# Output projection of a two-branch attention: split float32r products per row block, against float32 pieces of 128 columns behind P @ V

## The chip, the cores and the metric

The kernel runs on one NeuronCore of one Trainium2 chip. The metric is device time in microseconds (us), the median of several executions. The engines named here are TensorE (PE, its weight loads PEld), VectorE (DVE), ScalarE (ACT), GpSimd (POOL) and SyncE (SP), which issues nearly all DMAs. PSUM has eight banks, each of 128 partitions by 512 float32 columns.

## What is computed

The input is `x` with 2048 rows of 512, 32 heads of width 16. Branch A is plain softmax attention, branch B works on four chunks of 512 rows, causal inside a chunk, and mixes in a running memory of earlier chunks. Both have an output projection, and a gate mixes them:

```python
# A
p = softmax(q @ k.T * scale);  a = (p @ v) @ A_wo
# B, for each chunk s of 512 rows
a_dot = softmax(qs @ ks.T * scale + mask) @ vs
a_mem = (phi(qs) @ M) / (phi(qs) @ z + 1e-6)
o_s = sigmoid(beta) * a_mem + (1 - sigmoid(beta)) * a_dot
M, z = M + phi(ks).T @ vs, z + phi(ks).sum()
b = concat(o_s) @ B_wo
# both
g = sigmoid((x * gate_w).sum(-1));  out = g * a + (1 - g) * b
```

## The kernel before

**Stage 0** (lines 277 to 550) computes Q, K and V of both branches, the memory numerators and denominators of branch B, and the gates, and stores them in DRAM. At its end it also begins the row maxima.

**The slot loop** (lines 910 to 933) is all the rest. The work is cut into 64 units (`units`, line 99): side A or B, a group of four heads, a chunk of 512 query rows. A unit of side A has 64 slots, one of side B 10, 2368 slots in all, and 32 pairs of an A and a B unit of 74 slots each. One turn of the loop is one slot n and emits:

- `score_part(n)` (line 606): one score product into a bank of pool `st` (three banks), and ScalarE's exponential of that bank into a tile `p` (line 642, for two shapes 639).
- `max_part(n + 96)` (line 207): the product for the row maxima of a slot 96 later, into a bank of pool `sm` (four banks), and VectorE's reduction of that bank (line 219; for side B also 240, 244, and 230 to 234 by way of ScalarE and GpSimd). Score and maximum use different halves of the array's rows (heads at partitions 0 and 64), so a pair of them overlaps.
- every third slot (`BURST`), a burst: `some_values` (line 654) multiplies finished blocks of `p` by V. P @ V accumulates in one bank, `ops`, in float32, in four column tiles of the array: head h writes partitions 32h to 32h+16. A block is 128 query columns; up to four neighbours are one run of matmuls, so a run of w blocks is 4 heads x 128w columns, and each float32 matmul is two instructions. After it `run_late` (line 257) puts the transposed negated maxima into the query tile.

The program is written out by hand in this order. Each engine runs its own instructions in that order, so a matmul that waits for a bank holds everything behind it on TensorE.

**Beside it** stand steps given to a slot with `at(n, f)`. When a chunk of a side is done, its sums are loaded, inverted on VectorE, multiplied by the gate, stored, and loaded again as a factor broadcast over 16 partitions (`factors_at`, line 776; `value_load`, `factor_load`); GpSimd scales the values (`scale_part`, line 727) and adds the memory part (`memory_add`). The memory part is scaled ahead, stored to DRAM (`amd`) and loaded again.

**The projection** of chunks 0 to 2 is done per block of 128 rows. ScalarE makes the high part of the values in float32r (`out_hi`, 742), GpSimd the low part (`out_lo`, 747), for each side. `wo` was split the same way. Then `out_products` (line 750) makes 24 matmuls of 128x512 in three runs of eight (`RUN`), each into a bank of the score pool `st`, evacuated by ScalarE (760) and added by GpSimd (765). Each run of eight takes the place of P @ V in one burst (lines 926 to 932); the P @ V that was put off follows in the next. There are 4 blocks x 3 chunks x 3 = 36 such runs.

**The last chunk** goes by octets of eight heads (`piece`, line 834): six matmuls at a time into the four `sm` banks (line 890), in the last 88 or so slots, where there are no maxima any more. The octet of side A that ends last runs after the loop: its chain of DMAs, scale, split, 12 products and four copies out end the program.

Of the kernel before, what the change touches and what calls it, by code (L numbers as in the profile page):

```python
# [10 lines left out]
F32 = mybir.dt.float32  # L11
F32R = mybir.dt.float32r
# [25 lines left out]
RUN = 8  # L38
# [8 lines left out]
def gated_mix(ctx, tc, x, xT, wqkv, a_wo, b_wq, b_wk, b_wv, b_wo, beta, gate_w, out):  # L47
# [18 lines left out]
    amd = {c: dr.tile([128, NO, CH], F32, name=f"amd{c}") for c in range(1, NCH)}  # L66
# [18 lines left out]
    ogh = const.tile([128, 1], F32, name="ogh")  # L85
# [121 lines left out]
    def max_part(m, pool):  # L207
# [6 lines left out]
        ps = pool.tile([128, CH], F32, tag="sm", name="sm")  # L214
# [63 lines left out]
    with ExitStack() as p0:  # L278
# [145 lines left out]
        bt4 = wk1.tile([128, 1], F32, tag="bt4", name="bt4")  # L424
        nc.gpsimd.dma_start(bt4, beta.unsqueeze(1).unsqueeze(2).broadcast_to([H, 4, 1]))
# [87 lines left out]
        def some_max(place):  # L513
            m = mnext[0]
            if m == LEAD:
                return
            loads(m + 1 + PRE)
            for i in range(2):
                max_part(m + i, me_sm)
            run_todo(m + 1)  # L520
            mnext[0] += 2
            run_late(me_ps, "me", mnext[0])
# [31 lines left out]
    gate = {(s, c): gp.tile([128, 128], F32, name=f"g{s}{c}") for s in "AB" for c in range(NCH)}  # L554
    for (s, c), t in gate.items():
        nc.gpsimd.dma_start(t, gd["AB".index(s), c * CH:(c + 1) * CH].rearrange("(b t) -> b t", t=128)
                            .unsqueeze(0).broadcast_to([H, 4, 128]))
    gate_last = gp.tile([128, 32], F32, name="gateL")
    nc.gpsimd.dma_start(gate_last, gd[0, (NCH - 1) * CH:].rearrange("(q t) -> q t", q=16).unsqueeze(0).broadcast_to([8, 16, 32]))
# [6 lines left out]
    hl = ctx.enter_context(tc.tile_pool(name="hl", bufs=2, reuse_waits="tile"))  # L566
# [9 lines left out]
    def load_wo(side, w, t0):  # L576
        def load():
            wos["raw"] = fr.tile([128, NO, D], F32, tag="raw", name="woraw")
            nc.sync.dma_start(wos["raw"], w.rearrange("(o p) d -> p o d", p=128))
            wos[side] = [wo.tile([128, NO, D], F32R, name=f"wo{t}{side}") for t in "hl"]  # L580

        def split(o):
            h, l = wos[side]
            nc.gpsimd.tensor_copy(h[:, o], wos["raw"][:, o])
            nc.gpsimd.tensor_sub(l[:, o], wos["raw"][:, o], h[:, o].bitcast(F32))
        at(t0, load)
        for o in range(NO):
            at(t0 + 5 + 2 * o, lambda o=o: split(o))
# [13 lines left out]
    pt_ = {}  # L602

# [50 lines left out]
    def some_values(n, most=8):  # L654

        while queue and most and queue[0][0] <= n:
# [20 lines left out]
            if done:  # L677
                raw = ob.tile([128, CH], F32, tag="o", name="oraw")
                nc.scalar.copy(raw, ops)  # L679
                nc.sync.dma_start(od[side, c][4 * g:4 * g + 4].rearrange("h r t -> (h r) t"), raw)  # L680
                return


    held = {}

    def invert_load(side, c, src):
        t = fr.tile([128, 128], F32, tag="rec", name="rec", bufs=2)
        nc.sync.dma_start(t, src)
        held["rec", side, c] = t

    def recip(side, c, i, n=4):
        t = held["rec", side, c][:, i * 128 // n:(i + 1) * 128 // n]
        nc.vector.reciprocal(t, t)

    def invert(side, c):

        t = held.pop(("rec", side, c))
        if side == "B":
            nc.vector.scalar_tensor_tensor(t, t, ogh, gate["B", c], op0=ALU.mult, op1=ALU.mult)
        else:  # L700
            nc.vector.tensor_mul(t, t, gate["A" if side == "A" else "B", c])
        dst = rdM[c] if side == "M" else rd[side, c]
        nc.sync.dma_start(dst.rearrange("h (q t) -> (h q) t", q=4), t)
# [6 lines left out]
    TAG = {"A": "at", "B": "raw", "M": "am"}  # L710

    def big(key, tag):
        held[key] = fr.tile([128, NO, CH], F32, tag=tag, name=tag)
        return held[key]

    def value_load(side, c, o):
        if o == 0:
            big((side, c), TAG[side])
        nc.sync.dma_start(held[side, c][:, o], od[side, c][8 * o:8 * o + 8, 0:16].rearrange("h r t -> r h t"))

    def factor_load(side, c, o):
        if o == 0:
            big(("inv", side, c), "inv")
        nc.sync.dma_start(held["inv", side, c][:, o], heads((rdM[c] if side == "M" else rd[side, c])[8 * o:8 * o + 8]))

    def scale_part(eng, side, c, sl):
        eng.tensor_mul(held[side, c][sl], held[side, c][sl], held["inv", side, c][sl])

    def memory_load(c, o):
        if o == 0:  # L730
            big(("M", c), "am")
        nc.sync.dma_start(held["M", c][:, o], amd[c][:, o])

    def memory_add(eng, c, sl):
        eng.tensor_add(held["B", c][sl], held["B", c][sl], held["M", c][sl])

    def block(b):
        return np.s_[:, :, b * 128:(b + 1) * 128]

    def out_hi(c, b, side):  # L740
# [9 lines left out]
    def out_products(c, b, i):  # L750
# [10 lines left out]
        if i == 0:  # L761
            held["res", c, b] = t
            return
# [218 lines left out]
```

## Time and profile before

| | us |
|---|---|
| median of three runs | 2026.42 (2024.52 to 2027.84) |
| the profiled execution | 2020.79 |
| its span, first to last instruction | 2019.1 |
| TensorE busy | 1929.0 (96%) |
| VectorE busy | 1614.2 (80%) |
| ScalarE busy | 1485.6 (74%) |
| GpSimd busy | 364.0 (18%) |
| mean granted TensorE clock | 0.98 |

Busy times count the union of an engine's records. Matmul records overlap, because matmuls are pipelined, so a TensorE that is 96% busy may still be waiting inside a stretch that looks full; the distance from one start to the next tells more. A group's line gives the number of records, their union in us, the mean length of one in ns, and the idle time before them with what ended it. L675 is line 675 of the kernel. Stage 0 lasts to about 344 us of the span; then the slots begin.

### The profile page before, as it was taken

The numbers are of one execution on the slowest core, as the hardware profiler recorded it, in microseconds if no ns is written. First come the engines' busy times: TensorE is split into PE (matmuls) and PEld (weight loads), VectorE is DVE, ScalarE is ACT, GpSimd is POOL, SyncE is SP. The second block draws the span as 40 slices with busy tenths as digits, with TensorE's granted clock in tenths as the row PEclk, the third lists the DMA queues.
The fourth block names the chain that finished last, engine by engine and source line by source line (L and its number), as shares of the span: only waits on it lengthen the run. The fifth ranks groups of instructions, "written<-read, shape, count | busy, mean of one in ns | idle before, by whom it ended". The sixth has DMA issues, their size and how long they took to land.

```text
span 2019.1 us, 34830 instructions
## 1 busy us (share of the span) xinstructions
PE 1929.0 (96%) x12481; PEld 928.8 (46%) x12481; DVE 1614.2 (80%) x2740; ACT 1485.6 (74%) x2905; POOL 364.0 (18%) x566
## 2 busy tenths in 40 slices
PE   8999999999999999999999999999999999999996
PEld 6887765433433344444444444444444434444442
DVE  3235786998999999988888999888898998888800
ACT  3244333787888888878887888888887887877763
POOL 3000001233111112211121123111211232211240
PEclk9999998998999999999999999999998999999997
DMA  6668545355443337222221364223223552222311
GB/s 209 219 201 272 194 145 174 101 153 157 129 112 92 88 89 170 85 73 80 86 82 50 107 151 131 70 75 84 82 74 82 148 134 72 86 83 80 110 52 37
DMA packets 117483, 233.27 MB, mean 116 GB/s; under 512 B 24272, under 2 KB 38640, under 8 KB 116800
## 3 DMA queue, kind: packets, MB, share of 16 engines
q1 hardware_dynamic: 115792, 229.53, 39.1%
q8 instruction: 100, 1.64, 0.3%
q0 software_dynamic: 1232, 0.99, 0.2%
q14 instruction: 71, 0.58, 0.1%
q10 hardware_dynamic: 288, 0.52, 0.1%
HBM read 159.07 MB, written 70.66 MB: 114 GB/s over the span
## 4 chain that ended last, share of the span: by engine, by line
PE 81%; ACT 11%; DVE 4%; DMA 2%; issue 2%; POOL 0%; SPq 0%; ACTq 0%; DVEq 0%; POOLq 0%
PE ops L675 27%; PE st L619 26%; PE pr L311 12%; PE sm L204 9%; ACT p L642 8%; PE fin L758 4%; DVE pm L219 2%; PE fin L890 1%; ACT dg L230 1%; PE num L467 1%; ACT oraw L679 1%; PE mt_ps L194 1%; PE mps L498 0%; DMA qdA<-q 0%; DMA qdB<-q 0%
## 5 line engine op out<-in xcount | busy, mean ns | idle before, releaser
L219 DVE TENSOR_REDUCE pm<-sm 128x1 f32<-128x512 f32 x2048 | 1289.8, 682 | 156.8 <-PE sm L204 132.4
L642 ACT ACTIVATE p<-st 128x512 f32<-128x512 f32 x2304 | 1214.9, 609 | 211.7 <-PE sm L204 162.2
L619 PE MATMUL st<-qA,kA 50*128 50x512 f32 x2048 | 762.2, 454 | 36.2 <-ACT p L642 31.3
L204 PE MATMUL sm<-kA,qA 48*128 48x512 f32 x2048 | 785.0, 456 | 1.8 <-DVE pmB L240 0.8
L619 PEld LDWEIGHTS st<-qA,kA 50*128 50x128 f32 x2048 | 345.4, 188 | 597.7 <-ACT p L642 509.4
L675 PE MATMUL ops<-p,vA 128*17 128x512 f32 x4096 | 544.6, 607 | 0.0
L204 PEld LDWEIGHTS sm<-kA,qA 48*128 48x128 f32 x2048 | 343.9, 187 | 25.2 <-DVE pm L219 12.5
L204 PE MATMUL sm<-kB,qB 48*128 48x128 f32 (+2 forms) x896 | 176.2, 301 | 0.0
L204 PEld LDWEIGHTS sm<-kB,qB 48*128 48x128 f32 x896 | 138.4, 193 | 7.9 <-DVE pm L219 1.2
L619 PE MATMUL st<-qB,kB 50*128 50x384 f32 (+3 forms) x512 | 127.8, 348 | 12.6 <-ACT p L642 10.9
L675 PEld LDWEIGHTS ops<-p,vA 128*17 128x17 f32 x4096 | 69.9, 95 | 148.3 <-issue 137.2
L231 POOL TENSOR_SCALAR_AFFINE_SELECT dg<-dg 128x512 f32<-128x512 f32 x128 | 81.2, 635 | 277.8 <-ACT dg L230 277.6
L619 PEld LDWEIGHTS st<-qB,kB 50*128 50x128 f32 x512 | 73.9, 186 | 96.7 <-ACT p L642 81.0
L187 POOL CAST ms<-nm 128x16 fp32r<-128x16 f32 x64 | 12.6, 197 | 568.5 <-DVE nm L180 480.5
L359 DVE TENSOR_TENSOR q<-pr,q 128x512 fp32r<-128x512 f32 x64 | 44.0, 687 | 85.1 <-ACT q L352 76.7
L352 ACT CAST q<-pr 128x512 fp32r<-128x512 f32 x64 | 37.4, 585 | 94.9 <-PE pr L311 66.9
L623 POOL TENSOR_SCALAR_AFFINE_SELECT p<-p 128x512 f32<-128x512 f32 x128 | 78.5, 635 | 79.6 <-ACT p L642 77.2
L240 DVE TENSOR_REDUCE pmB<-sm 128x4 f32<-128x512 f32 x128 | 87.0, 680 | 5.3 <-PE sm L204 5.1
L675 PE MATMUL ops<-p,vB 128*17 128x512 f32 (+3 forms) x1024 | 89.5, 453 | 0.1
L234 DVE TENSOR_REDUCE pmB<-dg 128x4 f32<-128x512 f32 x128 | 86.7, 677 | 2.9 <-POOL dg L231 2.9
L230 ACT COPY dg<-sm 128x512 f32<-128x512 f32 x128 | 77.4, 605 | 5.7 <-DVE pmB L234 3.7
L765 POOL TENSOR_TENSOR res<-res 128x512 f32<-128x512 f32 x24 | 30.8, 1282 | 247.3 <-ACT res L760 247.3
(166 smaller groups left out, 1571.1 us busy)
## 6 DMA issues: line engine op xcount, KB each, us to landing
kA<-kdA SPq DMA_DIRECT2D x256, 128.0 KB
vA<-vdA SPq DMA_DIRECT2D x32, 544.0 KB
kA<-kdA SPq DMA_DIRECT2D x256, 64.0 KB
qdA<-q SPq DMA_DIRECT2D x32, 256.0 KB
kdA<-q SPq DMA_DIRECT2D x32, 256.0 KB
qdB<-q SPq DMA_DIRECT2D x32, 256.0 KB
qA<-qdA SPq DMA_DIRECT2D x64, 128.0 KB
kdB<-q SPq DMA_DIRECT2D x32, 256.0 KB
```

Of the source, the lines that this page charges most:

```text
L204: nc.tensor.matmul(ps[:, n0:n0 + n], rows(qt[u][:, :, s * 128:(s + 1) * 128], h, 48), rows(k[:, :, k0:k0 + n], h, 48), start=True, stop=True)
L219: nc.vector.tensor_reduce(pm[:, h, s, kc:kc + 1], ps, axis=AX.X, op=ALU.max)
L230: nc.scalar.copy(dg, blocked(ps))
L231: nc.gpsimd.affine_select(out=dg, in_=dg, pattern=[[0, 4], [-1, 128]], base=0, channel_multiplier=1, compare_op=ALU.is_ge, fill=MASKED)
L234: todo.append((m + MASK_T, lambda: nc.vector.tensor_reduce(to, dg.rearrange("p (h s) t -> p h s t", h=2), axis=AX.X, op=ALU.max)))
L240: nc.vector.tensor_reduce(pm[:, 1, h, 3:7], blocked(ps), axis=AX.X, op=ALU.max)
L311: nc.tensor.matmul(ps, l(a, k), r(b, k), start=(n == 0), stop=(n == 11))
L619: nc.tensor.matmul(ps[:, n0:n0 + CH - q0], rows(k[:, :, b * 128:(b + 1) * 128], h, 50), rows(q[:, :, q0:], h, 50), start=True, stop=True)
L623: nc.gpsimd.affine_select(out=x, in_=x, pattern=[[0, 4], [1, 128]], base=0, channel_multiplier=-1, compare_op=ALU.is_ge, fill=0.0)
L642: nc.scalar.activation(p[:, h], ps, AF.Exp, scale=SCALE)
L675: nc.tensor.matmul(ops[32 * h:32 * h + 17, q0:q0 + 128 * w], v[:, 17 * h:17 * h + 17], p[:, h, c0:c0 + 128 * w], start=(i == 0), stop=done ...
L758: nc.tensor.matmul(ps, l[:, o], r[:, o], start=(n == RUN * i), stop=(n == RUN * i + RUN - 1))
```

## The change

The projection is made in float32, without a split, in pieces. `piece(ps, side, o, c, b, j)` is one octet `o` of one side, one block `b` of 128 rows and 128 of the 512 output columns: four matmuls, one in each column tile, with 32 rows of values as weights and 128 columns of `wo` streamed past them. A block takes 8 octets x 4 = 32 pieces; the whole output 512 pieces, 2048 matmuls.

- The four `sm` banks become fixed tiles, used in rotation. A block of the projection takes one out of the rotation (`lent`) from its first piece to its last, so the maxima have three banks meanwhile. The score banks are no longer used for the projection.
- P @ V goes in every burst, at most three blocks of it (`MOST`), four where more than eight wait. A piece follows in the same burst, one per burst (two once there are no maxima), unless a transposed maximum is due. The program's order has 789 bursts with P @ V where it had 579, and 1161 runs of P @ V where it had 640.
- Chunks 0 to 2 start their pieces 24 slots after side A of the chunk ends. The last chunk's first octets (32 pieces) are made ahead, kept in SBUF (`keep`) and added at the end.
- The factors and values go by octet for all chunks (`octet`): a 128x32 reciprocal and product on VectorE, a store, a broadcast load, a scale on GpSimd. The memory part is no longer stored and loaded.
- Gone are: all splits of values and `wo`, the 36 copies and 24 additions of partial products.

By count of instructions in the program: DMA issues on SyncE 1513 to 1543, ScalarE 2907 to 2853, GpSimd 531 to 460, VectorE 2726 to 2754.

```diff
-RUN = 8
+MOST = 3
...
-    sm_ps = ctx.enter_context(tc.tile_pool(name="sm_ps", bufs=4, space=PSUM, reuse_waits="tile"))
+    sm_ps = ctx.enter_context(tc.tile_pool(name="sm_ps", bufs=1, space=PSUM, reuse_waits="tile"))
+
+    banks = [sm_ps.tile([128, CH], F32, name=f"sm{i}") for i in range(4)]
...
+    def octet(side, o, c, t0, vector=False):
...
+        def load():
...
+            nc.sync.dma_start(k["rec"], sums.rearrange("h (q t) -> h q t", q=16))
...
+            nc.sync.dma_start(k["v"], numd[c][:, o] if side == "M" else od[side, c][hs, 0:16].rearrange("h r t -> r h t"))
+
+        def factors():
+            nc.vector.reciprocal(k["rec"], k["rec"])
...
+            nc.sync.dma_start(rows.rearrange("h (q t) -> (h q) t", q=16), k["rec"])
+
+        def factor():
+            k["inv"] = fr.tile([128, CH], F32, tag="inv", name="inv", bufs=4)
+            nc.sync.dma_start(k["inv"], heads(rows))
+
+        def scale():
+            eng.tensor_mul(k["v"], k["v"], k["inv"])
+            if side == "B" and c:
+                eng.tensor_add(k["v"], k["v"], held["M", c][:, o])
+        for n, f in ((0, load), (10, factors), (17, factor), (28, scale)):
...
+    def piece(ps, side, o, c, b, j, start, stop):
+
+        for t in range(4):
+            nc.tensor.matmul(ps[32 * t:32 * t + 32, 128 * j:128 * j + 128],
+                             held[side, c][:, o, 128 * b + 32 * t:128 * b + 32 * t + 32], wos[side][:, o, 128 * j:128 * j + 128],
+                             start=start, stop=stop, tile_position=(0, 32 * t))
...
+    def block_fill(n, octets, c, b, then):
+
+        ks = [(side, o) for o in octets for side in "AB"]
+        for i in range(4 * len(ks)):
+            def f(i=i):
+                if i == 0:
+                    lent[c, b] = free.pop(0)
+                ps = banks[lent[c, b]]
+                piece(ps, *ks[i // 4], c, b, i % 4, i == 0, i == 4 * len(ks) - 1)
+                if i == 4 * len(ks) - 1:
+                    then(ps)
+                    free.append(lent[c, b])
+            fill.append((n, f))
+
+    def leave(c, b):
+        def then(ps):
+            t = fr.tile([128, D], F32, tag="res", name="res", bufs=2)
+            nc.scalar.copy(t, ps)
+            nc.sync.dma_start(out_rows(c, b), t)
+        return then
...
+                octet("M", o, c, seg_end["B", c - 1] + (60 if c > 1 else 0) + 14 * o)
+            for side in "AB":
+                if (side, o, c) != ("A", NO - 1, last):
+                    octet(side, o, c, end[side, 2 * o + 1, c] + 16)
+        if c < last:
+            for b in range(4):
+                block_fill(seg_end["A", c] + 24, range(NO), c, b, leave(c, b))
+    for b in range(4):
+        block_fill(nS - 208, range(1), last, b, keep(b))
...
-            filled[0] = bool(waiting) and not filled[0] and m < nS
-            if not filled[0]:
-                some_values(n)
-
-                run_late(st_ps, "st", m + 1)
-            if waiting and (filled[0] or m >= nS):
-                waiting.pop(0)()
+            some_values(n, MOST + (len(queue) > 8) if n < nS else 8)
+
+            if any(e[0] < m + 1 for e in late):
+                run_late(st_ps, "st", m + 1)
+            else:
+                for _ in range(1 if m < nS else 2):
+                    if filled[0] < len(fill) and fill[filled[0]][0] <= n:
+                        fill[filled[0]][1]()
+                        filled[0] += 1
         n += 1
...
+    octet("A", NO - 1, last, None, vector=True)
     for b in range(4):
+        for j in range(4):
+            close(0, "A", NO - 1, b, j)
+            fill.pop()[1]()
         t = fr.tile([128, D], F32, tag="res", name="res", bufs=2)
-        (nc.scalar.copy if b % 2 else nc.vector.tensor_copy)(t, fins[b])
-        (nc.scalar if b % 2 else nc.sync).dma_start(out[c * CH + b * 128:c * CH + (b + 1) * 128, :], t)
+        nc.vector.tensor_add(t, banks[b], part[b])
+        (nc.scalar if b % 2 else nc.sync).dma_start(out_rows(last, b), t)
```

More of the change, by code (lines that the diff above doesn't have):

```diff
@@ L680, in some_values @@
                 nc.sync.dma_start(od[side, c][4 * g:4 * g + 4].rearrange("h r t -> (h r) t"), raw)
+                stored.add(u)
                 return
[L684 to L703, printed above, removed]
@@ L726, in scale_part @@
[L726 to L740, printed above, removed]
-        h = hl.tile([128, NO, 128], F32R, tag="h" + side, name="h" + side)
-        nc.scalar.copy(h, held[side, c][block(b)])
-        held["hi", side, c, b] = h
@@ L745, in out_lo @@
[L745 to L767 removed]
+    held = {}
```

246 lines of the change are left out of this document (66 added, 180 removed).

## The prediction

> **What bounds the kernel now.** First the page's engine shares and its chain, then the stretches of the slot loop, then the chain inside one stretch.
>
> ```profile
> PE 1929.0 (96%) x12481; PEld 928.8 (46%) x12481; DVE 1614.2 (80%) x2740; ACT 1485.6 (74%) x2905; POOL 364.0 (18%) x566
> ...
> PE 81%; ACT 11%; DVE 4%; DMA 2%; issue 2%; POOL 0%; SPq 0%; ACTq 0%; DVEq 0%; POOLq 0%
> ```
>
> TensorE looks full, yet 15% of the chain is ScalarE and VectorE: it is held now and then. Next, the stretches, filtered to the tile `p`. The count behind the third busy time, ScalarE's, is that of exponentials, so of slots (two of them at the edges).
>
> ```profile
> 398.40:831.90 433.50, 177.88 (x1444) 25.07 (x1440) 348.92 (x668) 21.97 (x37) 0.99 0.44 121
> 831.90:1148.20 316.30, 115.80 (x964) 17.85 (x960) 233.40 (x446) 14.70 (x25) 0.99 0.28 80
> ...
> 1655.70:1874.80 219.10, 78.38 (x640) 11.81 (x640) 156.71 (x298) 10.80 (x18) 0.98 0.29 85
> 1874.80:1995.40 120.60, 42.72 (x344) 6.05 (x344) 78.27 (x148) 4.98 (x8) 0.97 0.20 54
> ```
>
> Without projection a slot takes 433.5/666 = 0.651 us. The second and third rows hold the projection of one chunk each, twelve runs of eight matmuls, and take 316.3/444 = 0.712 and 219.1/296 = 0.740. Over 0.651 that is 27 and 26 us, 2.2 us for each run. The chain shows what a run occupies, and what P @ V costs:
>
> ```profile
> 905.70 0.98 PE ops L675 x8
> 907.67 0.98 PE ops L675 x8
> 909.57 0.98 PE ops L675 x8
> 911.02 0.59 ACT p L642
> ...
> 913.14 0.98 PE ops L675 x8
> 914.60 0.59 ACT p L642
> 915.33 2.08 PE fin L758 x8
> ...
> 918.57 1.84 PE ops L675 x16
> ```
>
> A projection run takes 2.08 us and costs 2.2: it is paid in full. Where there is none, TensorE has slack. From 907.67 to 909.57, one burst of four blocks of P @ V and three pairs of score and maximum, it needs 1.90 us. But every fourth burst has no P @ V (909.57 to 913.14), and there ScalarE holds the scores. Twelve slots take 913.14 - 905.70 = 7.44 us, 0.620 a slot, where TensorE needs 3 x 1.90 and three bare pairs (1.90 - 0.98 = 0.92): 6.62. So the projection is charged in lumps, while 0.8 us of slack in each twelve slots is not used. What holds TensorE there is the pace of the engines behind it:
>
> ```profile
> L219 DVE TENSOR_REDUCE pm<-sm 128x1 f32<-128x512 f32 x2048 | 1289.8, 682 | 156.8 <-PE sm L204 132.4
> 904.83 3.07 DVE L219 TENSOR_REDUCE pm<-sm 128x1 f32<-128x512 f32 x5
> 909.12 1.58 ACT L642 ACTIVATE p<-st 128x512 f32<-128x512 f32 x3
> ```
>
> The first row is from the page's groups, the others from the order of time. Five reductions in 3.07 us, the last at its whole 0.68, are a stride of 0.598; three need 1.79 us. For exponentials, (1.58 - 0.59)/2 = 0.49; three need 1.47.
>
> **The change, part by part.** *A piece.* Four column tiles, two instructions each, 128 columns: the form of P @ V on one block, with 32 weight columns in place of 17. The sixteen instructions of 1.84 us less the eight of 0.98 give 0.86 for four blocks, so 0.215 for a block that follows others in the same tiling. A 128-column group with its fill and drain bounds it above:
>
> ```profile
> L194 PEld LDWEIGHTS mt_ps<-identf,ms 128*32 128x32 f32 x128 | 12.9, 113 | 39.5 <-issue 29.6 <-ACT p L642 8.1 <-ACT dg L230 0.9
> ...
> L675 PE MATMUL ops<-p,vB 128*17 128x128 f32 x256 | 12.8, 273 | 0.0
> ```
>
> 12.8 us for 32 groups of eight is 0.40. I take 0.215, since a piece stands behind P @ V, and add 0.01 a burst because 32 weight columns load in 113 ns against 107 (half of 215) of streaming. The split runs (1161 for 640) cost little by the order of time:
>
> ```profile
> 785.37 1.06 PE L675 MATMUL ops<-p,vB 128*17 128x384 f32 x16
> 786.36 0.50 PE L619 MATMUL st<-qA,kA 50*128 50x512 f32 x1
> ```
>
> 384 and 128 columns as two runs take 0.99 to the next score; four blocks in one run took 0.98: another 0.01.
>
> The Trainium skill, page "TensorE: Matmul & The Clock Gate", section "Back-to-back issue gap", speaks against the pieces: it gives about 81 ns for each load-and-multiply pair of 128 columns in sustained work. By that page eight such would be an estimated 0.65 us a piece, 0.43 more a burst, some 230 us more over 1600 slots and 2210 in all. The trace differs: its 128-column groups of eight take 0.40 at most.
>
> *A burst.* Three blocks and a piece stream as much as four blocks, so the 1.90 us stays, now in each burst: 1.92 with the two additions, 0.640 a slot. The rest of a slot (B's narrower products, transposed maxima) is 0.651 - 0.620 = 0.031. VectorE's 1.79 fits under 1.92, with little spare. The third pair of a burst starts about two thirds into the 0.92, at 0.6, and needs a free bank. With three banks that is the bank of the third maximum one burst earlier, whose reduction ends at about 0.5 (first product) + 2 x 0.598 + 0.68 = 2.38; it is wanted at 1.92 + 0.6 = 2.52. With four it would be the second's, done at 1.78. So extra VectorE work beyond some 0.14 us a burst is passed on to TensorE. There are two reductions for the negated maxima in each 74 slots, and 44 octets with a reciprocal and a product:
>
> ```profile
> L693 DVE RECIPROCAL rec<-rec 128x32 f32<-128x32 f32 x36 | 12.3, 343 | 0.0
> ...
> L182 DVE TENSOR_REDUCE nm<-pmB 128x16 f32<-128x64 f32 x32 | 6.7, 210 | 0.0
> ```
>
> 2 x 0.21 + 44/32 x (0.343 + 0.20, the product from the tail below) = 1.17 us in 74 slots, 0.016 a slot; with the spare I take 0.013. The bounds: below zero by up to 0.034 a slot, if B's extra 0.031 is hidden too; and 0.25 us a burst (0.083 a slot) if each third pair is held, estimated as half of a score's 0.50. I take the value near the VectorE rows. Sum: 0.640 + 0.031 + 0.013 = 0.684.
>
> *Slots 616 to 2220* carry it. Before: 124 slots at 0.651 and the stretch from 831.9 to 1874.8, 1042.9 us, together 1124. After: 1604 x 0.684 = 1097. Gain 27.
>
> *Slots before 616* have no pieces, but P @ V in each burst: 1.90 - 0.215 = 1.69, so VectorE sets the pace, as now. Even bursts gain (0.620 - 0.598) x 616 = 13 us at best, nothing at worst; I take 3, since 0.620 is near the stride already.
>
> *The last 148 slots* take 120.6 us, the last row of the stretches. The first 52 go to 0.684: 35.6 us. The other 96 have no maxima; their chain, and the tail's:
>
> ```profile
> 1971.77 0.98 PE ops L675 x8
> 1972.75 0.95 PE st L619 x3
> ...
> 1996.04 2.01 DMA odA<-oraw
> 1998.07 1.94 DMA rec<-odA
> 2000.63 1.72 DMA rdA<-rec
> 2002.40 3.31 DMA inv<-rdA
> 2007.23 4.57 PE fin L890 x10
> ```
>
> A burst there is 0.95 of scores, 0.98 - 0.215 of three blocks and two pieces of 0.23: 2.18 us, and 32 of them 70. Sum 105.5, gain 15. Some 28 pieces are left after the last P @ V, 6 us, under the DMAs that start at 1996.04 and end near 2006.
>
> ```profile
> 2000.41 0.20 DVE rec L854
> ...
> 2006.56 0.63 ACT hA L877
> ```
>
> *The tail* loses ScalarE's split (0.63). Its products took 4.57 us on a TensorE that had idled; 16 pieces at twice 0.215 would be 6.9, but each quarter goes out when it is done. Gain 2, between -2 and 4.
>
> *What I cost at nothing.* ScalarE loses 54 instructions, and its 1.47 lies under the 1.92. GpSimd loses 71. Behind a scale that waits for its factor stand the diagonal masks, and behind them P @ V of side B; but factor and scale are 11 slots (7.5 us) apart, against 3.31 us for the broadcast. SyncE issues 30 more, 1543; an octet's load may hold its queue for the 2.01 us of the store before it, and the key loads behind are issued 20 slots (13 us) ahead. VectorE's reciprocal stands 10 slots (6.8 us) behind its load, a store of 2.01 and a load of 1.94; without that cover VectorE stalls and, by the three banks, TensorE too.
>
> Together 27 + 3 + 15 + 2 = 47 us off the profiled execution's 2020.79: 1974. The median shown is 5.6 above that execution, so 1980.
>
> **The rivals.** *Three banks bind.* Where each third pair is held 0.25 us, a slot is 0.640 + 0.031 + 0.083 = 0.754, slots 616 to 2220 take 86 us more, and with 20 of other gains the time is 2092. It decides from 0.13 us a burst on (0.713 a slot uses up the 20). For it: the thin margin. Against: a held burst gives VectorE that time back.
>
> *A piece is paced by its instructions or weight loads*, not its columns: 0.40 by the upper row, a slot 0.745, 2078. It decides from 0.30 a piece. For it: weight loads of 113 ns against 107. Against: a split run costs 0.01. The Trainium skill's pace above is this mechanism taken further, and the upper row speaks against that much.
>
> *Banks and B's extra cost nothing*: 0.650 a slot, 81 us in the long stretch, 1925.
>
> *Nothing comes of it*: the lumps had covered waits that now return one by one, near 0.713.
>
> **How the numbers follow.** Forecast 0.62, three banks 0.16, paced pieces 0.08, no cost 0.10, nothing 0.04. Within 0.2% (4 us), about what a measurement can tell, lie the last and a sliver of the forecast: 0.05. Faster, 0.60 of the forecast and the no-cost case: 0.70. Slower, the two slow cases and another sliver: 0.25. The forecast's own range is 1945 to 2020; to leave out two in ten it goes from 1935 into the nearer half of the slow cases, 2055.
>
> **What would show it.** Pieces 0.21 to 0.24 us behind P @ V; bursts of one length near 1.95; a slot of 0.68 in the long stretch; few waits of the maxima for VectorE. The prediction is wrong if that wait is of hundreds of us, if a piece needs over 0.3, or if TensorE waits for GpSimd's scales.

## The result, and the profile after

| | before | after |
|---|---|---|
| median (lowest to highest) | 2025.47 us (2019.15 to 2027.84) | 1973.55 us (1969.92 to 1975.73) |
| profiled execution, its span | 2020.79, 2019.1 us | 1971.88, 1969.8 us |
| mean granted TensorE clock in it | 0.980 | 0.992 |
| VectorE, ScalarE busy | 1614.2, 1485.6 us | 1618.2, 1466.3 us |

Both medians are of four runs. The ratio is 0.9747, with a 95% interval of 0.9719 to 0.9775: 2.5% faster, where 1980 us and a range of 1935 to 2055 had been forecast. The page of the changed kernel has these engine shares, this chain and these groups:

```profile
PE 1932.7 (98%) x20361; PEld 1116.5 (57%) x20361; DVE 1618.2 (82%) x2768; ACT 1466.3 (74%) x2851; POOL 282.1 (14%) x497
...
PE 91%; DVE 3%; DMA 2%; ACT 2%; issue 1%; SPq 0%; DVEq 0%; ACTq 0%
...
L731 PE MATMUL sm<-woA,vA 128*32 128x128 f32 x2048 | 98.0, 279 | 6.5 <-DVE vA L719 6.5
```

TensorE's part of the chain has gone from 81% to 91%, ScalarE's from 11% to 2%. The matmuls of the pieces (line 731, one of two groups) are new. The same shows in what TensorE's weight loads waited for, first before, then after: us in total, times, longest.

```profile
PEld st L619 <- ACT p L642: 590.4, 1005, 1.7
...
PEld sm L204 <- DVE pm L219: 13.7, 43, 0.6
```

```profile
PEld st L610 <- ACT p L633: 236.4, 699, 0.7
...
PEld sm L203 <- DVE pm L218: 48.4, 178, 0.6
```

The scores wait less for ScalarE, and the maxima more for VectorE. Weight loads run beside matmuls, so these sums are larger than what they cost. One burst after the other, in order of time:

```profile
890.52 0.42 PE st L610
890.95 0.46 PE sm L203 x3
891.41 1.03 PE ops L666 x16
892.44 0.22 PE sm L731 x8
892.66 0.42 PE st L610
...
894.60 0.22 PE sm L731 x8
...
896.71 0.22 PE sm L731 x8
```

Each burst has its P @ V (`ops`) and behind it a piece (line 731) of 0.22 us, and the three pieces shown start 2.16 and 2.11 us apart. The stretches, filtered to the tile `p` as in the prediction, are now cut at slots 74, 592, 1036, 1184, 1628, 1776 and 2220; the last two rows are slots 616 to 2220 and 2220 to 2368. Behind the window stands its length; the count behind the third busy time is ScalarE's, and the number behind the fourth is the granted clock.

```profile
399.20:727.30 328.10, 145.40 (x2036) 40.98 (x2032) 272.94 (x519) 16.86 (x29) 1.00 0.38 105
727.30:1037.50 310.20, 124.62 (x1744) 35.07 (x1744) 235.65 (x446) 14.88 (x25) 1.00 0.37 101
1037.50:1131.70 94.20, 41.56 (x584) 11.71 (x584) 77.86 (x150) 5.22 (x9) 1.00 0.36 95
...
744.00:1843.50 1099.50, 450.26 (x6296) 126.63 (x6296) 850.48 (x1606) 53.73 (x87) 1.00 0.37 100
1843.50:1944.20 100.70, 41.55 (x580) 11.64 (x584) 77.70 (x148) 5.57 (x9) 1.00 0.17 49
```

The same cuts in the kernel before:

```profile
398.40:736.80 338.40, 139.65 (x1128) 19.48 (x1120) 271.61 (x519) 17.29 (x29) 0.98 0.41 117
736.80:1044.60 307.80, 116.39 (x960) 17.54 (x960) 233.40 (x446) 14.76 (x25) 0.99 0.36 97
1044.60:1148.20 103.60, 37.64 (x316) 5.90 (x320) 77.31 (x150) 4.62 (x9) 0.98 0.28 77
...
752.10:1874.80 1122.70, 425.16 (x3456) 62.06 (x3456) 844.22 (x1606) 54.00 (x88) 0.99 0.35 96
1874.80:1992.80 118.00, 41.66 (x336) 5.91 (x336) 77.67 (x147) 4.98 (x8) 0.97 0.20 55
```

The span is 49.3 us shorter. By stages, each from the exponentials' starts: the first exponential comes 4.3 us later (343.8 to 348.1), slots 0 to 616 take 12.4 us less (408.3 to 395.9), slots 616 to 2220 23.2 less, the last 148 slots 17.3 less, and the tail 0.7 less. Three things had to be explained. The stretch from slot 74 to 592 holds no projection and yet gains 10.3 us. With pieces a slot takes 310.2/444 = 0.699 us, in the gap behind them (slots 1036 to 1184, where a chunk's pieces have run out) 94.2/148 = 0.636. And the granted clock, at 0.97 to 0.99 in these rows before, is at 1.00.

### The profile page after: what moved, and what is told of

Its sections match the earlier page's. It is cut to its first block, busy times and chain, and to the rows that moved or that the text cites. A ratio compares the mean times of both kernels' runs of the same rounds, so it can differ in the third digit from the quotient of the medians.

```text
span 1969.8 us, 50626 instructions
## 1 busy us (share of the span) xinstructions
PE 1932.7 (98%) x20361; PEld 1116.5 (57%) x20361; DVE 1618.2 (82%) x2768; ACT 1466.3 (74%) x2851; POOL 282.1 (14%) x497
## 4 chain that ended last, share of the span: by engine, by line
PE 91%; DVE 3%; DMA 2%; ACT 2%; issue 1%; SPq 0%; DVEq 0%; ACTq 0%
PE ops L666 30%; PE st L610 26%; PE sm L203 16%; PE pr L310 12%; PE sm L731 5%; DVE pm L218 2%; ACT p L633 1%; PE num L467 1%; PE mps L498 1%; PE mt_ps L193 1%; DMA qdA<-q 0%; ACT dg L229 0%; DMA raw<-xT 0%; DMA qdB<-q 0%; PE tps L490 0%
## 5 line engine op out<-in xcount | busy, mean ns | idle before, releaser
L610 PE MATMUL st<-qA,kA 50*128 50x512 f32 x2048 | 701.7, 438 | 3.8 <-ACT p L633 3.6
L666 PE MATMUL ops<-p,vA 128*17 128x384 f32 (+1 forms) x8184 | 576.5, 384 | 0.0
L610 PEld LDWEIGHTS st<-qA,kA 50*128 50x128 f32 x2048 | 332.8, 186 | 273.4 <-ACT p L633 203.3
L666 PEld LDWEIGHTS ops<-p,vA 128*17 128x17 f32 x8184 | 165.0, 96 | 172.0 <-issue 161.7
L610 PE MATMUL st<-qB,kB 50*128 50x384 f32 (+3 forms) x512 | 119.9, 341 | 2.7 <-ACT p L633 2.3
L731 PEld LDWEIGHTS sm<-woA,vA 128*32 128x32 f32 x2048 | 66.5, 113 | 69.1 <-issue 43.3
L731 PE MATMUL sm<-woA,vA 128*32 128x128 f32 x2048 | 98.0, 279 | 6.5 <-DVE vA L719 6.5
L731 PEld LDWEIGHTS sm<-woB,vB 128*32 128x32 f32 x2048 | 64.7, 110 | 63.1 <-issue 45.3
L731 PE MATMUL sm<-woB,vB 128*32 128x128 f32 x2048 | 96.4, 273 | 0.0
L666 PE MATMUL ops<-p,vB 128*17 128x128 f32 (+3 forms) x1104 | 89.6, 417 | 2.9 <-issue 2.3
```

The lines of the kernel that those rows point to most:

```text
L610: nc.tensor.matmul(ps[:, n0:n0 + CH - q0], rows(k[:, :, b * 128:(b + 1) * 128], h, 50), rows(q[:, :, q0:], h, 50), start=True, stop=True)
L666: nc.tensor.matmul(ops[32 * h:32 * h + 17, q0:q0 + 128 * w], v[:, 17 * h:17 * h + 17], p[:, h, c0:c0 + 128 * w], start=(i == 0), stop=done ...
L731: nc.tensor.matmul(ps[32 * t:32 * t + 32, 128 * j:128 * j + 128], held[side, c][:, o, 128 * b + 32 * t:128 * b + 32 * t + 32], wos[side][: ...
```

## The experiments

Four theories stood against each other. (1) The even order of P @ V makes the gain, not the form or place of the projection. (2) The pieces make it: they use slack that lumps did not. (3) The bank lent by the maxima costs something that the pieces hide. (4) It is the granted clock.

### Even P @ V undone, alone and by itself

```diff
-            some_values(n, MOST + (len(queue) > 8) if n < nS else 8)
+            some_values(n, 8)
```

> The changed kernel with one part undone: P @ V waits again until four blocks can go together, up to eight in a burst, so that every fourth burst or so has none; the pieces stay where they are, one a burst. Theory 1 (the even P @ V is the gain): in the profile the stretch without pieces, slots 74 to 590, goes from 0.636 us a slot back to 0.645 to 0.655, the stretches with pieces from 0.697 to about 0.715 to 0.74, and the time lies 25 to 60 us above the changed kernel's 1973.6, at 2000 to 2035. Theory 2 (about half of the gain is granted clock): some ten of the 3.4 us windows at half clock come back behind bursts without P @ V, and the time that they take, the span times one less the mean clock, goes from 15.8 us to 30 to 45. Rival (evenness does not matter; the gain is the relief of ScalarE and GpSimd and the float32 pieces): the time stays within 5 us of 1973.6 and the clock at 0.99.

2022.64 us (2014.38 to 2031.28, ten runs); ratio to the kernel before 1.0008 (0.9982 to 1.0034). With uneven P @ V the whole change is worth nothing. Its stretches, at the same cuts:

```profile
396.30:733.40 337.10, 139.03 (x1128) 19.44 (x1120) 271.75 (x520) 17.41 (x29) 0.99 0.36 101
733.40:1052.70 319.30, 117.08 (x960) 16.67 (x960) 233.71 (x446) 14.70 (x25) 1.00 0.36 97
...
750.20:1881.00 1130.80, 422.44 (x3456) 59.97 (x3456) 842.73 (x1606) 53.40 (x87) 1.00 0.35 97
```

Without pieces 337.1 us where the changed kernel needs 328.1; with pieces 319.3 against 310.2. Theory 1 had asked for this. Theory 4 loses weight: the profiled execution, the fastest of the ten, has a clock of 0.993, as good as the changed kernel's 0.992, and its span is 42.5 us longer. The half-clock windows that had been expected did not come back: two of 3.4 us after slot 74, where the kernel before has twelve dips with 48 us in all.

What the uneven order does shows in slots 74 to 592, where there are no pieces. The weight loads of the scores waited for ScalarE (us in total, times, longest) in the kernel before, in this run and in the changed kernel:

```profile
PEld st L619 <- ACT p L642: 137.9, 235, 1.4
...
PEld st L610 <- ACT p L633: 137.5, 233, 0.9
...
PEld st L610 <- ACT p L633: 91.7, 205, 0.7
```

With P @ V uneven the scores are held some 46 us longer, whichever way the projection is made. The sum is larger than its price, 9 to 10 us of this stretch, for the reason told above. It agrees with the prediction's reading that ScalarE holds the scores in the bursts without P @ V.

The opposite edit is to the kernel before, one line:

```diff
-                some_values(n)
+                some_values(n, 3 + (len(queue) > 8) if n < nS else 8)
```

> The kernel before with one part of the change alone: P @ V goes in each burst, at most three blocks, four where more than eight wait. The projection stays as it was, 36 runs of eight float32r products, each in the place of a burst's P @ V, and the maxima keep four banks throughout. Theory (evenness carries the gain in the long stretch, and the pieces only pay for the lent bank): the stretch without projection goes from 0.653 to 0.633 us a slot, slots 616 to 2220 from 1122.7 to about 1604 x 0.636 + 36 x 2.2 = 1099, as in the changed kernel, and the last 148 slots stay at 118; 1985 to 1995. Rival (the two parts are worth something only together, since runs of eight in the place of P @ V unsettle an even order again): 2005 to 2025.

1966.66 us (1964.21 to 1975.22); ratio 0.9721 (0.9672 to 0.9769). That is 18 us below what was expected, and no slower than the changed kernel. In slots 74 to 592 its scores waited 91.9 us for ScalarE, as in the changed kernel:

```profile
401.40:728.00 326.60, 145.45 (x2036) 40.98 (x2032) 272.71 (x519) 16.94 (x29) 1.00 0.41 121
728.00:1024.00 296.00, 122.19 (x1680) 34.14 (x1680) 234.50 (x445) 15.20 (x25) 1.00 0.37 100
...
743.00:1824.40 1081.40, 443.17 (x6104) 124.70 (x6104) 849.00 (x1606) 53.75 (x87) 1.00 0.35 99
1824.40:1938.60 114.20, 42.42 (x580) 11.81 (x584) 77.71 (x149) 5.64 (x9) 0.99 0.24 63
```

The two runs and the two kernels make a table of medians (us):

| | split runs of eight | float32 pieces, lent bank |
|---|---|---|
| uneven P @ V | 2025.5 | 2022.6 |
| even P @ V | 1966.7 | 1973.6 |

The order of P @ V decides, whichever way the projection is made. In an even order the pieces lose 18.1 us in slots 616 to 2220 (1099.5 against 1081.4) and win 13.5 back in the last 148 slots (100.7 against 114.2).

### What a piece costs, and what the bank

First the pieces of chunks 0 to 2 were left out, with the bank lent as before:

```diff
-                piece(ps, *ks[i // 4], c, b, i % 4, i == 0, i == 4 * len(ks) - 1)
+                if c == last or i in (0, 4 * len(ks) - 1):
+                    piece(ps, *ks[i // 4], c, b, i % 4, i == 0, i == 4 * len(ks) - 1)
```

> The changed kernel without the pieces of chunks 0 to 2, but for the first and the last of each block, so the output of these chunks is left out; the bank is lent for as long as before. It shows what three banks cost by themselves. If they cost nothing, the stretches in which a bank is lent run at 0.63 to 0.64 us a slot, as where none is lent, and the time is 1973 less 372 pieces by 0.18, near 1906. If they bind, these stretches stay at 0.66 to 0.70 and the time at 1930 to 1970; waits of the maxima's products for VectorE then stay at 40 us or more.

1932.67 us in one execution. 360 pieces are gone (the expectation counted 372), and only 35.9 us in slots 616 to 2220. The banks do bind: the stretches with a lent bank run at 297.5/444 = 0.670, those without at 0.636. Then the pieces were put into another bank, so that the maxima keep four:

```diff
+                if c < last:
+                    side, o = ks[i // 4]
+                    j = i % 4
+                    for t in range(4):
+                        nc.tensor.matmul(ops[32 * t:32 * t + 17, 128 * j:128 * j + 128],
+                                         held[side, c][:, o, 128 * b + 32 * t:128 * b + 32 * t + 17], wos[side][:, o, 128 * j:128 * j + 128],
+                                         start=False, stop=False, tile_position=(0, 32 * t))
...
+                    return
                 if i == 0:
                     lent[c, b] = free.pop(0)
```

> The changed kernel with the pieces of chunks 0 to 2 added into the bank of P @ V instead of a lent one, 17 weight columns each in place of 32, so that the maxima keep four banks; they come one a burst while a unit of side A is open. The output of chunks 0 to 2 and the values of side A are spoilt by that; only the time counts. It tells the price of a piece with four banks. The run without pieces showed 0.670 us a slot with three banks and 0.636 with four, against 0.697 with three banks and pieces. If the pieces cost their 0.2 us wherever they stand, a slot with pieces is 0.636 + 0.06 = 0.695 here too, and three banks cost nothing once pieces are there: 1965 to 1975. If the lent bank is part of the price, a slot with pieces is 0.660 to 0.680: 1930 to 1955.

1934.85 us in one execution, inside the second range. A line not shown lets a piece in only while a unit of side A is open in the bank of P @ V. And the fourth corner, neither pieces nor lending:

```diff
-                if i == 0:
+                if c < last and i < 4 * len(ks) - 1:
+                    return
+                if i == 0 or c < last:
                     lent[c, b] = free.pop(0)
                 ps = banks[lent[c, b]]
-                piece(ps, *ks[i // 4], c, b, i % 4, i == 0, i == 4 * len(ks) - 1)
+                piece(ps, *ks[i // 4], c, b, i % 4, i == 0 or c < last, i == 4 * len(ks) - 1)
```

> The changed kernel without the pieces of chunks 0 to 2 (one piece a block is left, so the output of these chunks is left out) and without the lending: the fourth corner beside three banks without pieces (1063.6 us for slots 616 to 2220), four banks with pieces (1064.4) and three with pieces (1099.5). If the stretches of these slots run like the gaps between the pieces, 1604 x 0.636 = 1020 us and a time near 1890, then the bank costs 44 us by itself, the pieces 44 by themselves, and both together 79. If the steps of the octets, which lie in these slots, hold the four banks too, 1035 to 1060: then part of what looked like the bank's price is theirs.

1897.02 us in one execution. What the edits of these single executions don't touch repeats closely: slots 74 to 592 take 328.0, 328.1 and 328.2 us, and 328.1 in the changed kernel. Slots 616 to 2220 of the three, in the order told:

```profile
739.90:1803.50 1063.60, 450.29 (x6296) 126.65 (x6296) 849.45 (x1605) 53.49 (x87) 1.00 0.37 103
```

```profile
741.70:1806.00 1064.30, 450.18 (x6296) 126.65 (x6291) 852.24 (x1605) 53.46 (x87) 1.00 0.37 103
```

```profile
742.30:1768.80 1026.50, 450.28 (x6296) 126.76 (x6296) 845.64 (x1605) 53.72 (x87) 1.00 0.39 107
```

| slots 616 to 2220, us | four banks | three banks |
|---|---|---|
| no pieces | 1026.5 | 1063.6 |
| pieces | 1064.3 | 1099.5 |

The two prices nearly add up: the bank costs 37.1 us without pieces and 35.2 with them, the pieces 37.8 us with four banks and 35.9 with three. The runs do not hold quite the same pieces, though. In these slots the changed kernel has 385 and the run with four banks 356, with 17 weight columns each in place of 32, and the runs without pieces still have 27 (three banks) and 16 (four). So a piece costs 35.9/358 = 0.10 us with three banks and 37.8/340 = 0.11 with four, where it occupies TensorE for 0.22: about half of it lies in slack in both. With 29 more pieces at 0.11 the run with four banks would be some 3 us longer, which leaves 32 us for the bank with pieces, an estimate. Theory 2 is right in that spread pieces use slack, and theory 3 in its first half only: the lent bank costs, and the pieces hide little of it. The octets' steps, the rival in the last expectation, explain little: 1026.5/1604 = 0.640 against 0.636 in the gaps. Where the bank's price arises, the waits in the first stretch with pieces (slots 592 to 1036) show, three banks first, four second, both without pieces:

```profile
PEld sm L203 <- DVE pm L218: 15.2, 56, 0.7
```

```profile
PEld sm L203 <- DVE pm L218: 6.0, 24, 0.5
```

That is 9.2 us more of waiting for VectorE's reductions in a stretch that is 13.3 us longer (297.5 against 284.2). In the same stretch the scores' weight loads waited 11.1 us less for ScalarE (66.9 against 78.0), so these sums show the place of the price, not its size.

Each piece of chunks 0 to 2 made twice gives the price of a second one in a burst:

```diff
-                piece(ps, *ks[i // 4], c, b, i % 4, i == 0, i == 4 * len(ks) - 1)
+                piece(ps, *ks[i // 4], c, b, i % 4, i == 0, c == last and i == 4 * len(ks) - 1)
+                if c < last:
+                    piece(ps, *ks[i // 4], c, b, i % 4, False, i == 4 * len(ks) - 1)
```

> The changed kernel with each piece of chunks 0 to 2 made twice in its burst, which doubles their output. It gives the slope of the second piece. If the first piece stands partly in the wait for the lent bank (0.027 us a slot, so 0.08 a burst, by the run without pieces), the second has nothing left to hide in and costs its 0.22 us: 0.697 + 0.073 = 0.770 us a slot with pieces, 384 x 0.22 = 84 us more, about 2057. If a piece costs 0.08 us whichever it is, 0.725 a slot and about 2005.

2024.74 us in one execution, between the two forecasts. Slots 616 to 2220 take 1153.1:

```profile
742.80:1895.90 1153.10, 450.25 (x6296) 126.57 (x6296) 851.46 (x1606) 53.75 (x87) 1.00 0.34 96
```

53.6 us for 384 pieces is 0.14 each: dearer than the first, and still not paid in full.

### Spread or in lumps, float32 or split

The same pieces, eight at once in each eighth burst:

```diff
-                for _ in range(1 if m < nS else 2):
+                k = 1 if m < nS else 2
+                if m < nS:
+                    ahead = filled[0] + credit[0]
+                    credit[0] += ahead < len(fill) and fill[ahead][0] <= n
+                    k = credit[0] if credit[0] == 8 else 0
...
+                for _ in range(k):
```

> The changed kernel with the same pieces of chunks 0 to 2, but eight of them at once in each eighth burst instead of one in each burst; P @ V stays even. The prediction held that lumps are paid in full and that spread pieces use slack. If so, eight pieces at once cost 8 x 0.218 = 1.74 us for what costs 8 x 0.18 when spread: 384/8 = 48 lumps by 0.3 us, plus 5 to 25 us, 1979 to 1998. Rival (the spreading is the gain): the stretches with pieces go from 0.697 to 0.72 or more, plus 45 us, near 2020. Rival (the pieces are paid in full either way): within 4 us of 1973.6.

1997.10 us (1994.81 to 1998.10), ratio 0.9868 (0.9842 to 0.9894): 23.5 us more than spread, the first forecast's upper end. Slots 616 to 2220 take 1125.0, so a lump of eight costs 25.5/48 = 0.53 us more than eight spread pieces. Over the 1063.6 without pieces that is 61.4/360 = 0.17 us a piece, against 0.10 spread and 0.22 occupied. Spreading does help, if by less than the order of P @ V.

The products of the kernel before one at a time, spread in the same way, with even P @ V and a lent bank:

```diff
     def out_products(c, b, i):
...
         if i == 0:
...
+            lent[c, b] = free.pop(0)
+        ps = banks[lent[c, b]]
...
+        nc.tensor.matmul(ps, l[:, o], r[:, o], start=(i == 0), stop=(i == 23))
```

> The kernel before with its split values and float32r products, but P @ V even as in the changed kernel (at most three blocks in each burst), the four maxima banks fixed with one lent to a block, and one product of 128x512 behind the P @ V of each burst, 24 for a block, which accumulate in the lent bank; the last chunk as before. It keeps the even P @ V and the lent bank and drops the float32 pieces in column tiles. Theory 1 (evenness is the gain, whatever the form of the product): a product costs an estimated 0.26 us (2.08 for a run of eight), 24 of them 6.2 us a block against 32 x 0.218 = 7.0, so the long stretch is as fast as the changed kernel's or up to 10 us faster, and only the last 148 slots give back their 15 us: 1970 to 1995. Rival (the float32 pieces in the tiles of P @ V are the gain, since a switch of tiling costs): near the kernel before, 2010 to 2025.

2004.54 us (2001.92 to 2008.67), ratio 0.9908 (0.9880 to 0.9937). Slots 616 to 2220 take 1114.1, 14.6 more than with float32 pieces. So theory 1 in its strict form, whatever the form of the product, falls: spread and with a lent bank, 128 columns in the tiling of P @ V are the better form. A product costs (1114.1 - 1026.5)/288 = 0.30 us, 7.3 a block, and a block of pieces 73.0/12 = 6.1; both hold the price of the lent bank, and both are estimates, since the factors' steps differ. For these products spreading did not pay: in runs of eight, with the same even P @ V and four banks, these slots took 1081.4, which is 32.7 less. That is near the price of a lent bank, 37.1. The last 148 slots, as before the change in this kernel, take 117.2.

### A burst in every second slot

```diff
-BURST = 3
-MOST = 3
+BURST = 2
+MOST = 2
```

> The changed kernel with a burst in every second slot instead of every third, at most two blocks of P @ V (three where more than eight wait) and one piece each. The pieces then need 768 slots of a lent bank in place of 1152, and the bursts are shorter, so that a bank is back before it is wanted. TensorE's need of a burst is 2 x 0.306 for the pairs, 2 x 0.215 + 0.12 for P @ V, 0.218 for a piece: 1.38, with 0.031 a slot for B 0.72 a slot with a piece. If that is all, slots 616 to 2220 take 768 x 0.72 + 836 x 0.636 = 1085 instead of 1099.5: 1955 to 1965. Rival (each switch between the forms of product costs TensorE more than the bank gives back): 0.75 a slot with pieces, 0.65 without, 1990 to 2010.

2005.56 us (2004.43 to 2005.81), ratio 0.9902 (0.9867 to 0.9937): the rival. The stretch without pieces rises to 335.2/518 = 0.647 and slots 616 to 2220 to 1124.1. There are half as many bursts again, and with them switches between the forms of product; that these are what costs fits the numbers, and was not tested by itself.

### A mixture

Even P @ V, split runs in a score bank for chunks 0 to 2, float32 pieces (with `wo` loaded a second time) for the last chunk. Of this edit, the order inside a burst:

```diff
+            put = bool(waiting) and not put
+            if put:
+                waiting.pop(0)()
+            else:
+                some_values(n, MOST + (len(queue) > 8) + 2 * (len(queue) > 10) if n < nS else 8)
```

> A mixture that the runs so far point to: even P @ V and, for chunks 0 to 2, the split float32r products in runs of eight in a score bank in the place of one burst's P @ V (36 runs, spread over the whole of the next chunk), so that the maxima keep four banks; for the last chunk the float32 pieces of the changed kernel. By the stages: slots 616 to 2220 as in the kernel before with even P @ V, 1081 us; the last 148 slots as in the changed kernel, 101; start and tail as in the changed kernel: 348 + 396 + 1081 + 101 + 26 = 1952, 1945 to 1960. If the even order alone does not carry the long stretch, and the late chunk or the splits on GpSimd disturb it, 1965 or more.

> The same with runs of four instead of eight: 72 runs of 4 x 0.26 = 1.04 us, near the 0.98 of a P @ V of four blocks, each in the place of one burst's P @ V, with 36 more copies on ScalarE and additions on GpSimd. If what counts is that all bursts are alike, the runs use more of TensorE's slack (0.03 us a slot in the stretch without projection) and the long stretch is 5 to 20 us shorter than with runs of eight: 1930 to 1948. If a run costs by its TensorE time whatever its length, the same time within 4 us; if each switch of form costs, 5 to 10 us more.

2019.47 us (ratio 0.9980, 0.9957 to 1.0002) and 2019.59 us (0.9987, 0.9968 to 1.0005): no gain over the kernel before in either, where 1945 to 1960 and 1930 to 1948 had been expected, and no difference between runs of eight and of four. Both had the octets' steps bunched, two octets in every ten slots, since their buffers were single. What VectorE and then TensorE did at the worst place of the first of them, in order of time and by windows over all instructions (length, then TensorE's busy time; the clock is the third number from the end):

```profile
753.82 0.35 DVE L719 RECIPROCAL rec<-rec 128x32 f32<-128x32 f32 x1 [5.60 <-DMA rec<-odA]
```

```profile
744.00:749.00 5.00, 5.00 (x50) 2.42 (x42) 4.19 (x9) 3.54 (x7) 0.00 (x0) 1.00 0.74 204
749.00:755.00 6.00, 0.04 (x1) 0.00 (x0) 1.15 (x4) 1.18 (x3) 1.26 (x1) 0.67 0.44 109
755.00:785.00 30.00, 26.16 (x135) 11.44 (x137) 16.47 (x33) 11.21 (x21) 8.39 (x11) 0.50 0.67 172
```

A reciprocal waited 5.60 us for its load, behind other octets' stores and loads on SyncE; the reductions behind it held the maxima's banks, TensorE stood for 6.0 us, and the clock was half for 30 us more. Spreading the steps tests this:

```diff
-octet(side, o, c, max(end[side, 2 * o + 1, c] + 16, (seg_end["A", c] + 16 if c < last else seg_end["A", last - 1] + 330) + 10 * o + 5 * (side == "B")))
+octet(side, o, c, max(end[side, 2 * o + 1, c] + 16, (seg_end["A", c] + 16 if c < last else seg_end["A", last - 1] + 334) + 24 * o + 12 * (side == "B")))
```

> The mixture with runs of eight once more, but the steps of the octets (load, reciprocal, factor, scale) 12 slots apart instead of 5, and the memory's octets 140 slots later, after the others. In the mixture before, TensorE stood for 6.0 us at 749, 4.4 at 1178, 3.1 at 1587 and 5.0 at 1822 us, where many octets' steps fell together, behind reductions that stood behind reciprocals whose loads were late, and half clock followed each time. Theory (the bunch of steps, not the runs of products, cost the mixture its gain): these stalls go, slots 616 to 2220 come to 1075 to 1090 and the time to 1945 to 1960. Rival (the mixture's spread runs cost more than those of the kernel before with even P @ V): the long stretch stays above 1110, 1980 or more.

In the same edit the memory's octets come up to 140 slots later, and the runs of products begin 48 slots later and stand closer together. 1966.02 us (1964.56 to 1967.58), ratio 0.9721 (0.9704 to 0.9737). The stalls are gone: the longest wait of the maxima for a reduction is 0.8 us, where it was 6.5. So the bunched steps had cost the 53 us; which of the shifts did it was not tested by itself. But the long stretch (1096.6) and the time lie 6 us above what was expected: the runs cost 15 us more here than in the kernel before with even P @ V, and why stays open. The mixture is no better than that one-line edit, 1966.66.

## Why the prediction was right, step by step

**The sum was right, its main reason was not.** The prediction said that "the projection is charged in lumps, while 0.8 us of slack in each twelve slots is not used", and credited the gain to pieces that use it. The slack was there and the pieces do use it (0.10 us for 0.22). But with the bank that they borrow they are no cheaper than the runs. Measured in the prediction's way, with slots 74 to 592 as the base, slots 616 to 2220 held 1122.7 - 1604 x 0.653 = 75 us of projection before, 2.1 us a run, and hold 1099.5 - 1604 x 0.633 = 84 us now. The gain is the 32 us by which the rest of these slots got shorter, and by the two one-line edits that is the even order: with pieces in both runs, and no dip of the clock in either, the uneven order costs 1130.8 - 1099.5 = 31.3 us in these slots. A run costs (1081.4 - 1604 x 0.631)/36 = 1.9 us in the even order too, by the same measure. Over the run with neither pieces nor lending, 1026.5, it would be 1.5, but that base was not measured in an uneven order. (All these are estimates, since the factors' steps differ.)

The prediction named the even order's worth only for the slots before 616, and put it at 3 us, where the one line is worth 57 in all. That its total still came out owes something to luck.

**A piece**, 0.215 forecast: right. Eight records take 0.22 in the order of time. The pace of 81 ns a pair, quoted in the prediction from the Trainium skill, page "TensorE: Matmul & The Clock Gate", section "Back-to-back issue gap", is not this trace's: 0.22 us for eight pairs are 27 ns a pair.

**A burst**, 1.92 with 0.031 a slot for B, so 0.671 a slot where TensorE sets the pace: right for four banks, where 0.667 was measured with pieces in most bursts (slots 592 to 1036 took 296.3 us).

**VectorE's extra work passed on by three banks**, 0.013 a slot: mis-sized. The bank costs 0.670 - 0.640 = 0.030 a slot, 0.09 us a burst, between the term and its upper bound of 0.083 a slot. The first rival had the mechanism right and a price of 0.25 us a burst that is three times too high; it stayed below the 0.13 from which it would have decided.

**Slots 616 to 2220**, a gain of 27 forecast, 23.2 measured: two errors that cancel. A slot with pieces takes 0.699 instead of 0.684, and the bursts shown start 2.16 and 2.11 us apart instead of near 1.95. And the prediction put pieces in all 1604 slots, where a chunk's pieces run out before the next chunk's begin: two gaps of about 173 slots run at 0.636.

**Slots before 616**, 3 forecast within 0 to 13: 12.4, near the bound. "0.620 is near the stride already" was read off twelve slots, though the prediction's own first row had 0.651; slots 74 to 592 gave 0.653 before and 0.633 after.

**The last 148 slots**, 15 forecast, 17.3 measured: right. **The tail**, 2 forecast, 0.7: right within its bounds; its 16 pieces took longer on an idle TensorE, but each quarter left as soon as it was done. The first exponential came 4.3 us later, which no step had; in the experiments built on the changed kernel it came between 344.5 and 348.2 us, so most of it is no effect of the change.

**What was costed at nothing** held in the main: P @ V waited 4.1 us in all for GpSimd's masks, and no reciprocal waited for its load while there were maxima. One did in the last slots, 29.2 us until 1911.6, when VectorE had no reductions left to do. What that cover is worth the first mixture showed.

## What to carry to other kernels

When a stretch is paced by several engines by turns, first make the turns alike: one line that spread P @ V was worth 57 us (2023.8 to 1966.7), and the rebuilt projection nothing beside it. Price both forms of a piece of work in the better order before one replaces the other: here the lumps, 1081.4 us for slots 616 to 2220, beat the pieces, 1099.5. A bank taken from a rotation has its own price, and it is found by taking the bank without the work.

## What the runs showed of the hardware

The granted clock fell behind windows in which TensorE was busy most of the time. In the kernel before, over all instructions (length, TensorE's busy time; the clock third from the end):

```profile
868.10:871.50 3.40, 3.40 (x30) 0.86 (x22) 2.27 (x5) 2.02 (x5) 0.60 (x1) 1.00 0.00 0
871.50:874.90 3.40, 2.80 (x25) 1.47 (x25) 2.95 (x6) 3.09 (x8) 0.63 (x1) 1.00 0.00 0
874.90:878.30 3.40, 3.40 (x20) 1.58 (x18) 1.68 (x4) 1.54 (x4) 0.00 (x0) 0.50 0.37 102
```

The window ahead of the dip is 2.80 of 3.40 us busy, but it falls on a burst without P @ V: only 0.15 us of its time has P @ V matmuls, against 2.56 in the window before. In the next 3.4 us a run of eight P @ V matmuls takes 1.91 us, where one before it took 1.05:

```profile
870.56 1.05 PE L675 MATMUL ops<-p,vA 128*17 128x512 f32 x8
...
874.86 1.91 PE L675 MATMUL ops<-p,vA 128*17 128x512 f32 x8
```

The Trainium skill, page "TensorE: Matmul & The Clock Gate", section "What's actually happening", gives such a window, 3413 ns, and the same half rate after an idle one; the length and the rate agree with these rows, the idleness does not.

The clock changes on a grid of 3.41 us, on which the loop of the kernel before, from 360 us on, has 475 windows. In 14 of them the matmuls of P @ V and of the projection take 0.40 us or less together, and behind 11 of these the clock is half. Behind the other 461 it is half four times, twice as the second window of a longer dip. So these dips go with windows that have hardly any of these matmuls; the three such windows without a dip show that this is not the whole rule.

Thirteen such dips, 51 us in all, lie in the loop of the kernel before, and none between 360 us and the end of the loop of the changed one. At half rate they can have cost at most half of that, 25 us. How much of the 49 us they are is not shown by a run of its own. Over 47 executions of the kernel before, taken beside the experiments, the span rises by 0.73 us for each us of span times one less the mean clock; by that the dips would be some 19 us, an estimate from a correlation. They are not all of it: the run with uneven P @ V and pieces had 6.8 us of them after slot 74, and its profiled execution was 42.5 us longer than the changed kernel's.

The second finding is that the prices of a bank and of the pieces nearly added up (37 and 38 us alone, 73 together). A wait and a piece of work on the same engine might have covered each other; here they hardly did, and why was not tested.
